# The first batch's row scatters without their marks: an FFT and mixture-of-experts kernel on one core

## The chip, the core and the metric

The kernel runs on one core of a Trainium2 chip. The metric is the device time of one execution in microseconds (us), the median over the runs shown. The core has a matrix engine (TensorE, PE in the rows; its weight loads are PEld), a vector engine (VectorE, DVE), a scalar engine (ScalarE, ACT), a general engine (GpSimd, POOL) and a queue engine (SyncE, SP). Each engine works through its own list of instructions in order and waits for the others by semaphores. DMA transfers are issued by SP and by POOL in this kernel and run on 16 DMA engines.

## What is computed

```python
# x: 8 batches x 2496 positions x 256 channels
X = np.fft.fft(np.fft.fft(x, axis=1), axis=2).real       # 19968 tokens of 256
logits = X @ w_gate + modality_bias[modality_id]          # 8 experts
e_idx = np.argmax(logits, axis=1)
gate_w = softmax(logits)[e_idx]
for e in range(8):
    mask = e_idx == e
    h = np.maximum(X[mask] @ w1[e], 0.0)                  # 256 -> 1024
    out[mask] = gate_w[mask, None] * (h @ w2[e])          # 1024 -> 256
```

## The kernel before

**Three strands of work share the engines.** (1) The transform, batch by batch (b = 0 to 7): loads `XM`, folds on VectorE (L402, L499 to L511), small matrix products into PSUM tiles `psf` (`stage1` L556 and L558, `stage23` L582 to L604), copies out of them (`T`, L524, L532, L533, L594), rows `rp` of a pair of frequencies and their mirrored rows `rm` (`Group.data`, L222 and L223), each 3 x 516 values of 16 bits for 117 partitions. (2) The weights: 16 loads of 1 MB (`wa`, L977), squares for a bound (`wj`, `wst`, L988), a scale (`web`, `wsc`), a split into a high and a low half-precision part (`w`, L1020 on ScalarE and L1021 on VectorE), and a store back to memory (L972). (3) The experts' blocks: 128 or 256 tokens of one expert, `psm` <- `xT`, `w` (L1236, four PSUM tiles of twelve products for 256 tokens), their two halves `H` (ScalarE L1241, then VectorE L1242), `pso` <- `w`, `H` (L1259; the pool has one buffer), the scaled result `ob` (L1266) and a scatter of it to `out` by POOL (L1267).

**Routing.** `route` takes the logits of a batch and gives each row its place `dsti` among its expert's rows (L745). A row then gets its token number and gate value as a `tail` of four 16-bit values (`Group.rows`, two copies at L235 for a group of up to three rows). `scatter` (L817) writes one column of a group, 117 rows, to its places in the table `xd` in memory, by an indirect DMA on POOL. A batch has 22 scatters. Batch 0 is routed in two parts, after 6 and after all 11 of its row columns, which gives 12 and 10 scatters. A block reads its tokens from `xd` by a DMA transpose on SP (`xT`, L1220) and a small load (`ig`, L1223), which wait until all scatters of the batches in question have landed (`drain`). The first three blocks of 128 tokens, named here by their experts 0 to 2, take their rows from SBUF by a one-hot product instead (`onchip`, L798) and don't read `xd`; the fourth is the first that does.

**Who sends the scatters.** In the first stretch (up to the end of the list `SEQ` in `fft_moe`) a scatter goes out through `paced`: one call after each step of the transform and after each half block, and behind a half block that `SEQ` names up to three more as long as the next scatter is of batch 0. `paced` takes the next scatter and adds a dependency on `self.mark`, the latest VectorE instruction of the kind "low half of a product read from PSUM" that the program had written by then (`evac` L533 or `H` L1242). It then calls `rows()` of the group that comes next, so that its tail copies stand in VectorE's list. Later batches use `trickle`, or `paced` with the same marks.

**What sets the order.** The order in which instructions stand on each engine is not written by hand. The program is recorded, and a scheduler with its own model of times lays the instructions out by their dependencies, so a dependency more or less also moves instructions on engines that it doesn't name. POOL's DMAs use eight completion counters in turn: each DMA waits until the one eight before it has landed.

The construction that the diff touches is printed here with its callers.

Of the kernel before, what the change touches and what calls it, by code (L numbers as in the profile page):

```python
# [239 lines left out]
class Pads:  # L240

    b, list = B - 1, None
# [8 lines left out]
class Kernel:  # L251
# [590 lines left out]
    def paced(self):  # L842

        if not self.pend:
            return
        mark = self.mark
        self.next_scatter()
        self.tc.add_manual_dep(self.scattered, mark.name, mybir.DependencyInfo(
            mybir.DependencyClass.Sync, mybir.DependencyReason.DATA), reason="spreads the scatters in time")
        for group, _ in self.pend[:1]:  # L850
            group.rows()

# [589 lines left out]
```

## Time and profile before

| what | before |
|---|---|
| median of 3 runs | 1032.28 us (1031.05 to 1039.42) |
| the profiled execution | 1028.82 us |
| its span, first to last instruction | 1026.8 us |
| TensorE matmul busy, share of the span | 994.3 us, 97% |
| VectorE busy | 560.1 us, 55% |
| ScalarE busy | 446.3 us, 43% |
| POOL busy | 375.9 us, 37% |

The profiled execution is one run; its span leaves 2.0 us outside (start and end). A busy time is the union of an engine's instructions. Matrix products overlap their neighbours in the records, so a busy PE may still be a waiting one, and its waits are read from the rows that give idle time. In a row of the timeline the bracket says how long the engine stood idle before the instruction and which instruction's signal ended that by the trace's inference; where an instruction had other waits too, the name is that of the last to come.

### The profile page before, as it was taken

The page shows a single profiled execution, that of the slowest core. Times are in us where ns is not written, and L with a number is a line of the kernel's source. Part 1 is how long each engine was busy: PE and PEld are TensorE (multiplying, and loading weights), DVE is VectorE, ACT ScalarE, POOL GpSimd, SP SyncE. Part 2 cuts the span into 40 slices and gives each one's busy share as a digit, 9 for nine tenths or more (in the row PEclk, how much of TensorE's full clock was granted, in tenths as well). Part 3 has the DMA queues.
Part 4 walks back from the last instruction along what each step waited for, and adds up shares of the span by engine and source line. Part 5 has one row for each costly group of instructions (what it writes and reads, how often), then busy time and mean ns, then how long its engine had stood idle before and what let it go on. Part 6 is the DMA issues. An engine that isn't in the chain of part 4 may idle for free.

```text
span 1026.8 us, 26338 instructions
## 1 busy us (share of the span) xinstructions
PE 994.3 (97%) x10033; PEld 896.7 (87%) x10033; DVE 560.1 (55%) x1670; ACT 446.3 (43%) x890; POOL 375.9 (37%) x353
## 2 busy tenths in 40 slices
PE   8688999999999999999999999999999999999996
PEld 5587988899999999998999899988888888899995
DVE  4996989675878744955375634553232222222221
ACT  6776788444445333533353333333232323223331
POOL 0245384355245343443344243334444212121111
PEclk9989999999999999999999999999999999999999
DMA  9777997699599798549764954879797986597870
GB/s 333 286 276 261 240 389 255 189 335 308 198 323 265 230 290 208 146 130 308 223 160 132 288 151 111 238 220 255 207 269 220 349 238 160 167 320 137 209 210 22
DMA packets 152018, 237.66 MB, mean 231 GB/s; under 512 B 115820, under 2 KB 118901, under 8 KB 133709
## 3 DMA queue, kind: packets, MB, share of 16 engines
q1 hardware_dynamic: 132509, 193.75, 64.6%
q0 software_dynamic: 19376, 42.16, 13.0%
q8 instruction: 81, 1.33, 0.5%
q14 instruction: 52, 0.43, 0.1%
HBM read 206.37 MB, written 60.48 MB: 260 GB/s over the span
## 4 chain that ended last, share of the span: by engine, by line
PE 80%; issue 6%; DMA 5%; DVE 4%; ACT 2%; POOL 2%; SPq 0%; POOLq 0%; DVEq 0%; ACTq 0%
PE pso L1259 37%; PE psm L1236 36%; PE psf L582 2%; DMA xd<-rm,dsti 2%; PE psf L602 2%; PE psf L556 2%; DMA wa<-w 1%; POOL out L1267 1%; POOL xd L817 1%; DMA XM<-x 1%; ACT wj L988 1%; DVE w L1021 1%; ACT w L1020 1%; DMA ig<-xd 1%; PE psf L587 0%
## 5 line engine op out<-in xcount | busy, mean ns | idle before, releaser
L1236 PE MATMUL psm<-xT,w 128*128 128x256 f16 (+1 forms) x4512 | 457.7, 258 | 5.1 <-ACT xT L801 1.5
L1259 PE MATMUL pso<-w,H 128*128 128x256 f16 x3864 | 451.4, 273 | 0.6 <-ACT ob L1266 0.6
L1236 PEld LDWEIGHTS <-w 128*128 128x128 f16 x4512 | 386.8, 98 | 43.9 <-issue 4.6
L1259 PEld LDWEIGHTS <-H 128*128 128x128 f16 x3864 | 374.0, 98 | 43.6 <-issue 0.7
L1242 DVE SCALAR_TENSOR_TENSOR H<-psm,H 128x512 f16<-128x512 f32 x322 | 219.9, 688 | 322.8 <-ACT H L1241 322.6
L1267 POOL DMA_INDIRECT out<-ob,ig x161 | 165.4, 1028 | 432.8 <-ACT ob L1266 372.2
L1241 ACT ACTIVATE H<-psm 128x512 f16<-128x512 f32 x322 | 190.8, 598 | 237.1 <-PE psm L1236 235.7
L1266 ACT ACTIVATE ob<-pso,gs 128x256 f32<-128x256 f32 x161 | 69.2, 471 | 259.1 <-PE pso L1259 241.4
L817 POOL DMA_INDIRECT xd<-rp,dsti x88 | 99.1, 1126 | 127.3 <-issue 29.8
L817 POOL DMA_INDIRECT xd<-rm,dsti x88 | 99.8, 1134 | 56.1 <-issue 18.9
L533 DVE SCALAR_TENSOR_TENSOR T<-psf,T 120x280 f16<-120x280 f32 (+2 forms) x95 | 43.2, 464 | 70.2 <-ACT T L532 70.1
L532 ACT ACTIVATE T<-psf 120x280 f16<-120x280 f32 (+2 forms) x95 | 38.6, 424 | 8.5 <-PE psf L582 5.1
L988 ACT ACTIVATE wj<-wa 128x1024 uint8<-128x1024 f32 x32 | 34.1, 1065 | 8.1 <-DMA wa<-w 8.0
L602 PE MATMUL psf<-T,pack 120*117 120x145 f16 x330 | 33.5, 224 | 0.0
L582 PE MATMUL psf<-pack,T 128*120 128x144 f16 (+1 forms) x330 | 32.2, 230 | 0.0
L1021 DVE SCALAR_TENSOR_TENSOR w<-wa,wsc,w 128x1024 f16<-128x1024 f32 (+1 forms) x16 | 28.9, 1807 | 2.4 <-ACT w L1020 2.4
L602 PEld LDWEIGHTS <-pack 120*117 120x117 f16 x330 | 27.9, 133 | 0.6
L587 PE MATMUL psf<-m2u,T 128*120 128x280 f32 x88 | 25.5, 418 | 1.9 <-DVE web L411 1.1
L582 PEld LDWEIGHTS <-T 128*120 128x120 f16 x330 | 26.9, 133 | 0.5
L402 DVE TENSOR_TENSOR XM<-XM 128x1280 f32<-128x1280 f32 (+2 forms) x18 | 23.7, 1337 | 6.4 <-DMA XM<-x 6.4
L604 PEld LDWEIGHTS psf<-T,pack 120*117 120x117 f32 x132 | 19.5, 188 | 8.1 <-ACT T L524 4.3
L604 PE MATMUL psf<-T,pack 120*117 120x145 f32 (+1 forms) x132 | 22.8, 296 | 2.9 <-ACT T L524 1.4
(216 smaller groups left out, 664.2 us busy)
## 6 DMA issues: line engine op xcount, KB each, us to landing
w<-w SPq DMA_DIRECT2D x87, 1028.0 KB
w<-w SPq DMA_DIRECT2D x87, 1024.0 KB
XM<-x SPq DMA_DIRECT2D x14, 1280.0 KB
wa<-w SPq DMA_DIRECT2D x16, 1024.0 KB
out<-ob,ig POOLq DMA_INDIRECT x161
XM<-x SPq DMA_DIRECT2D x2, 768.0 KB
xT<-xd SPq DMA_TRANSPOSE x91
xd<-rp,dsti POOLq DMA_INDIRECT x88
```

Source lines behind the costliest of these rows:

```text
L533: self.mark = self.nc.vector.scalar_tensor_tensor(dst[:, 1], ps, scale, dst[:, 0], ALU.mult, ALU.subtract).ins
L582: nc.tensor.matmul(oh, T1[h][:, a, g, :], self.m2h[h][:, w], start=h + k == 0, stop=h * k == 2, skip_group_check=True)
L602: nc.tensor.matmul(ps3[0:M3, cols], self.e3h[:, a, j, :], T2[:, w, cols], start=k == 0, stop=k == 2)
L604: nc.tensor.matmul(ps3[0:M3, cols], self.e3[:, j, :], T2[:, cols], start=True, stop=True)
L817: i = self.nc.gpsimd.indirect_dma_start(out=self.t["xd"], out_offset=bass.IndirectOffsetOnAxis(ap=at, axis=0), in_=row, in_offset=None, bo ...
L988: nc.scalar.activation(jk, x, AF.Square, accum_out=st[:, i:i + 1])
L1236: l1 = nc.tensor.matmul(ps[:, q, :], w1v[:, h, kt, ft], xT[:, xs, :], start=k == 0, stop=k == 5).ins
L1241: nc.scalar.activation(H[:, 0, f0:f0 + NF, :], ps, AF.Relu)
L1242: self.mark = V.scalar_tensor_tensor(H[:, 1, f0:f0 + NF, :], ps, 0.0, H[:, 0, f0:f0 + NF, :], ALU.max, ALU.subtract).ins
L1259: nc.tensor.matmul(po[:, tg, :], H[:, hh, ft, tg * P:(tg + 1) * P], w2v[:, wh, ft, :], start=k == 0, stop=k == 23)
L1266: self.ob = nc.scalar.activation(ob, po[:, tg, :], AF.Identity, scale=gs[:, tg:tg + 1]).ins
L1267: ins = nc.gpsimd.indirect_dma_start(out=t["out"], out_offset=bass.IndirectOffsetOnAxis(ap=ig.bitcast(I32)[:, tg, 0:1], axis=0), in_=ob, i ...
```

## The change

`paced` still takes one scatter per call, at the same calls, and still lets `rows()` of the next group follow. Only where the scatter is of batch 0 it no longer adds the dependency on the mark.

```diff
-        mark = self.mark
+        mark, b = self.mark, self.pend[0][0].b
         self.next_scatter()
-        self.tc.add_manual_dep(self.scattered, mark.name, mybir.DependencyInfo(
-            mybir.DependencyClass.Sync, mybir.DependencyReason.DATA), reason="spreads the scatters in time")
+        if b:
+            self.tc.add_manual_dep(self.scattered, mark.name, mybir.DependencyInfo(
+                mybir.DependencyClass.Sync, mybir.DependencyReason.DATA), reason="spreads the scatters in time")
```

From L848 on the changed kernel's lines are one higher (L1242 before is L1243 in it). The lists of the five engines are the same, but for that shift, up to the first block that reads `xd` on TensorE (about 100 us into the run) and from about 200 us on; POOL's differ from its first scatter on.

POOL's list from its first scatter, before (names: `xd<-rp,dsti` and `xd<-rm,dsti` are scatters, `out<-ob` the results of a block; the number after `ig` tells the blocks apart):

```order
L817 DMA xd<-rp,dsti 162048x516 x3
L817 DMA xd<-rm,dsti 162048x516 x3
L817 DMA xd<-rp,dsti 162048x516 x3
L817 DMA xd<-rm,dsti 162048x516 x4
L817 DMA xd<-rp,dsti 162048x516 x2
L817 DMA xd<-rm,dsti 162048x516 x2
L1267 DMA out<-ob,ig_575 19968x256
L1267 DMA out<-ob,ig_762 19968x256
L817 DMA xd<-rp,dsti 162048x516 x2
L817 DMA xd<-rm,dsti 162048x516 x2
L817 DMA xd<-rp,dsti 162048x516
```

and in the changed kernel:

```order
L817 DMA xd<-rp,dsti 162048x516 x3
L817 DMA xd<-rm,dsti 162048x516 x3
L817 DMA xd<-rp,dsti 162048x516 x3
L817 DMA xd<-rm,dsti 162048x516 x3
L1268 DMA out<-ob,ig_575 19968x256
L817 DMA xd<-rp,dsti 162048x516 x2
L817 DMA xd<-rm,dsti 162048x516 x3
L817 DMA xd<-rp,dsti 162048x516 x2
L817 DMA xd<-rm,dsti 162048x516 x2
L1268 DMA out<-ob,ig_762 19968x256
L817 DMA xd<-rp,dsti 162048x516
```

Both lists hold the 22 scatters of batch 0. The first block's result (`ig_575`) moved from behind seventeen of them to behind twelve, and the second block's (`ig_762`) from behind seventeen to behind twenty-one.

TensorE's list at the end of the block `H_1540` (the third that reads `xd`), before. `pso<-w_2_125,H_1540` is that block's second product, `psf<-m2q,T_1716` a step of the transform, `psm<-xT_2169` the first product of the block after next:

```order
L1259 LDWEIGHTS H_1540
L1259 MATMUL pso<-w_2_125,H_1540 128x256
L593 MATMUL psf<-m2q,T_1716 120x2x80 x2
L1259 LDWEIGHTS H_1540
L1259 MATMUL pso<-w_2_125,H_1540 128x256
L1259 LDWEIGHTS H_1540
L1259 MATMUL pso<-w_2_125,H_1540 128x256
L1259 LDWEIGHTS H_1540
L1259 MATMUL pso<-w_2_125,H_1540 128x256
L1236 LDWEIGHTS w_1_121
L1236 MATMUL psm<-xT_2169,w_1_121 128x256
```

and in the changed kernel:

```order
L1260 LDWEIGHTS H_1540
L1260 MATMUL pso<-w_2_125,H_1540 128x256
L592 MATMUL psf<-m2p,T_1715 120x2x72
L593 MATMUL psf<-m2q,T_1716 120x2x80 x2
L1260 LDWEIGHTS H_1975
L1260 MATMUL pso<-w_0_123,H_1975 128x256
```

Eight products of the next block (`H_1975`) into the one `pso` buffer now stand ahead of the first product of `xT_2169`; before, 24 of those came first.

ScalarE's list from the first `H` of the block `H_1975`, before (`w<-wa` and `w<-wf` are weight splits, `wj` squares, `T` copies of the transform):

```order
L1241 ACTIVATE H_1975<-psm 128x512
L1020 ACTIVATE w_0_123<-wa,wsc 128x2048
L1241 ACTIVATE H_1975<-psm 128x512
L524 COPY T_1715<-psf 128x11x36
L1020 ACTIVATE w_1_121<-wf,wsc 128x1024
L1020 ACTIVATE w_1_121<-wa,wsc 128x1024
L524 COPY T_1715<-psf 128x11x24
L524 COPY T_1716<-psf 128x11x36
L1241 ACTIVATE H_1975<-psm 128x512
```

and in the changed kernel:

```order
L1242 ACTIVATE H_1975<-psm 128x512
L1021 ACTIVATE w_0_123<-wa,wsc 128x2048
L1021 ACTIVATE w_1_121<-wf,wsc 128x1024
L1021 ACTIVATE w_1_121<-wa,wsc 128x1024
L524 COPY T_1715<-psf 128x11x36
L524 COPY T_1715<-psf 128x11x24
L1021 ACTIVATE w_1_124<-wa,wsc 128x2048
L989 ACTIVATE wj,wst<-wa 128x1024
L524 COPY T_1716<-psf 128x11x36
L1242 ACTIVATE H_1975<-psm 128x512
```

The second `H` of that block moved from behind one weight split to behind four and a square. The result `ob` of the block `H_1540` comes, in both lists, after the four `H_1975`, four weight splits, four copies `T` and two squares; before, two more copies (`L594`) stood ahead of it.

## Rows read from the trace of the kernel before

**Rows 1.** The page: engines' busy time, and the granted clock in 40 slices.
```profile
PE 994.3 (97%) x10033; PEld 896.7 (87%) x10033; DVE 560.1 (55%) x1670; ACT 446.3 (43%) x890; POOL 375.9 (37%) x353
PEclk9989999999999999999999999999999999999999
```
**Rows 2.** Stretches: busy time (instructions) of PE, PEld, DVE, ACT, POOL; clock, DMA.
```profile
40.00:60.00 20.00, 15.07 (x230) 14.51 (x231) 19.60 (x60) 14.22 (x24) 7.68 (x6) 0.91 0.52 189
60.00:80.00 20.00, 17.21 (x200) 15.78 (x198) 18.76 (x72) 14.08 (x23) 11.57 (x8) 0.91 0.90 321
...
121.20:132.90 11.70, 11.70 (x111) 10.75 (x110) 11.70 (x41) 11.70 (x18) 8.65 (x6) 1.00 1.04 318
...
400.00:500.00 100.00, 100.00 (x989) 90.54 (x987) 59.62 (x177) 40.46 (x83) 38.89 (x37) 1.00 0.69 204
```
**Rows 3.** POOL's timeline: start, us, what, [idle before <- what ended it].
```profile
45.48 2.30 POOL L817 DMA_INDIRECT xd<-rp,dsti  x1 [18.06 <-DVE rm L235]
...
54.06 0.99 POOL L817 DMA_INDIRECT xd<-rm,dsti  x1 [0.30 <-issue]
66.30 0.99 POOL L817 DMA_INDIRECT xd<-rp,dsti  x1 [11.25 <-DVE pcv L812]
...
72.29 3.01 POOL L817 DMA_INDIRECT xd<-rm,dsti  x1 [0.30 <-issue]
...
78.08 1.11 POOL L817 DMA_INDIRECT xd<-rm,dsti  x1 [0.30 <-issue]
...
94.84 1.25 POOL L817 DMA_INDIRECT xd<-rp,dsti  x1 [0.82 <-DMA out<-ob,ig]
```
**Rows 4.** VectorE's timeline: tail copies, the second part's places, two weight splits.
```profile
40.19 0.15 DVE L235 COPY rm<-tail 117x6 int32<-117x6 int32 x1
...
45.22 0.15 DVE L235 COPY rm<-tail 117x6 int32<-117x6 int32 x1
...
57.83 2.34 DVE L1021 SCALAR_TENSOR_TENSOR w<-wa,wsc,w 128x2048 f16<-128x2048 f32 x1
...
74.04 0.15 DVE L745 CAST dsti<-dst 117x10 int32<-117x10 f32 x1
...
74.58 2.33 DVE L1021 SCALAR_TENSOR_TENSOR w<-wa,wsc,w 128x2048 f16<-128x2048 f32 x1
```
**Rows 5.** SP's timeline of DMA issues: two weight loads, the first transpose.
```profile
43.07 2.06 SPq L977 DMA_DIRECT2D wa<-w  x1
...
99.35 1.32 SPq L1220 DMA_TRANSPOSE xT<-xd  x1
...
135.59 0.45 SPq L977 DMA_DIRECT2D wa<-w  x1
```
**Rows 6.** TensorE's timeline: the waits behind which the argument stands, and one place between.
```profile
102.19 2.84 PE L1236 MATMUL psm<-xT,w 128*128 128x128 f16 x48 [0.61 <-DMA xT<-xd]
...
131.00 2.78 PE L1236 MATMUL psm<-xT,w 128*128 128x256 f16 x24
...
147.57 0.16 PE L422 MATMUL psf<-wst,ones 128*128 128x1 bf16 x1 [1.13 <-ACT wj L988]
...
162.33 0.51 PE L592 MATMUL psf<-m2p,T 128*120 128x144 f32 x2 [0.94 <-DVE xeb L411]
...
164.47 0.83 PE L1236 MATMUL psm<-xT,w 128*128 128x256 f16 x6 [0.92 <-DVE xsc L413]
```
**Rows 7.** ScalarE's timeline.
```profile
50.62 1.06 ACT L988 ACTIVATE wj<-wa 128x1024 uint8<-128x1024 f32 x1 [2.08 <-DMA wa<-w]
...
131.31 0.73 ACT L594 COPY T<-psf 120x280 f32<-120x280 f32 x2
...
132.92 0.54 ACT L1266 ACTIVATE ob<-pso,gs 128x256 f32<-128x256 f32 x1
...
146.37 1.06 ACT L988 ACTIVATE wj<-wa 128x1024 uint8<-128x1024 f32 x1 [2.15 <-DMA wa<-w]
```
**Rows 8.** DMA from 40 to 100 us: POOL's queue, packets, MB, share of 16 engines.
```profile
q0 software_dynamic: 1504, 2.84, 14.0%
```

## The prediction

> **What bounds the kernel now.** I read the page first, then the stretches, then the waits of TensorE one by one, and last what POOL does.
>
> TensorE is busy 994.3 of 1026.8 us [rows 1]. Busy is not yet working at its pace, but in the stretch from 400 to 500 us it is busy throughout at the full clock while VectorE has 59.6 and ScalarE 40.5 us of work in 100 [rows 2], and its timeline shows no wait there. So whatever happens early, from about 200 us on the rest is a fixed amount of matrix work. The change can move the end only by what it does to TensorE's waits before that. They lie early: in 40 to 60 us TensorE is busy 15.1 of 20 us, in 60 to 80 us 17.2, at a mean clock of 0.91 [rows 2]. Behind 100 us four waits are worth naming: 0.61 us for the first transposed tokens at 102.19, 1.13 us for a product over weight squares at 147.57, 0.94 us at 162.33 and 0.92 us at 164.47 [rows 6]. Together 3.6 us. That is the first thing to see: a gain beyond about 10 us has nowhere to come from in the stretch that the change can reach.
>
> Now POOL. The first scatter of batch 0 starts at 45.48, the sixth at 54.06, the seventh at 66.30 after 11.25 us of idle time, the thirteenth at 78.08, the last at 94.84 [rows 3]. Two of these waits are marks: the first scatter's group had its tail copies at 40.19 and the second group's at 45.22 [rows 4], 5 and 21 us before its first scatter went out. SP issues the first transpose at 99.35 [rows 5], 3.3 us behind the end of the last scatter's instruction (94.84 + 1.25 = 96.09), and TensorE takes it up at 102.19, 2.8 us later [rows 6].
>
> **What the change does, step by step.**
>
> *The scatters go out sooner.* The first six can start behind the copy at 40.19 + 0.15, five us sooner, the second six behind the first instead of at 66.30, so twelve are out near 60 us instead of 78. The second part's ten can't start before their places, cast at 74.04 + 0.15 [rows 4]; before, their first went at 78.08 because POOL was still busy with the first part. From 74.2, with the first held up to about 77 as the one at 72.29 was, then nine scatters and one block result at 1.3 us (the pitch of a 0.99 us scatter with the 0.30 us between two, [rows 3]), the last ends at 77 + 10 x 1.3 = 90 us, and 91 with one more held up. That is 5 us sooner than 96.1.
>
> *What the 5 us are worth.* The transpose follows the last landing, so TensorE could have its tokens at about 102.2 - 5 = 97. It arrives for them at 101.58 (102.19 less 0.61) and its list before that place is unchanged, so it can gain 0.61 us and no more. **Term 1: -0.6** (bounds -0.6 and 0). The other 4.4 us are slack. If the scatters came out no sooner than before, that term would be 0.
>
> *The scatters' packets.* POOL's 24 DMAs from 40 to 100 us (22 scatters, 2 results) took 14.0% of 16 DMA engines [rows 8], 0.14 x 60 / 24 = 0.35 us of all engines each. The load of weights at 43.07 [rows 5] is late already: ScalarE stood 2.08 us for it until 50.62 [rows 7]. About three scatters more fall in front of its landing, so it can come 0 to 3 x 0.35 = 1.0 us later, and ScalarE has little slack there. The DMA engines are busy only 0.52 of the stretch, so I take less than half. **Term 2: +0.4** (0 to +1.0). The other end gains nothing: from 60 to 80 us the engines are 0.90 busy [rows 2] and six scatters leave that stretch, but none of TensorE's waits there is for a load.
>
> *VectorE beside POOL.* More scatters now lie beside VectorE's long instructions. In the trace the scatter is the one that pays: 3.01 us at 72.29 instead of 0.99 [rows 3], while the weight split at 74.58, with a scatter across its start and another one inside, took 2.33 us, and the same one at 57.83 with no scatter near it 2.34 [rows 4]. **Term 3: 0.** The Trainium skill, SBUF — State Buffer, section "Who interferes with whom", says that the two engines lock a shared port pair for a whole instruction and that whichever issues first blocks the other; by that rule scatters could also hold VectorE up. The rows agree for one direction only. Its further inference, that an operation with two SBUF inputs doesn't hold up descriptor writing, is not what the 3.01 us suggest.
>
> *The lists that the scheduler moved.* The dependency that is gone moved work between 100 and 200 us on TensorE, VectorE and ScalarE; each list keeps the same work. Two places matter. At the first, TensorE now has eight products of `H_1975` ahead of the products of `xT_2169`. They need the one `pso` buffer, so they wait for `ob` of the block before, on ScalarE. Before, ScalarE needed from the first `H_1975` (just before 121.20) to that `ob` at 132.92 [rows 7] 11.7 us without a gap (busy 11.70 of 11.70 us, [rows 2]). In the new list the same instructions stand ahead of it, less the two copies of 0.73 us, so 11.0 us, and its own half us makes 11.5: with the 0.6 us of term 1 it is done at 121.2 - 0.6 + 11.5 = 132.1. TensorE came to this place at 131.00 [rows 6], so now at 130.4, and stands 1.7 us. Before, the 24 products covered this. If ScalarE loses as much again to VectorE's small steps the wait is 3.4, if the copies in front also shorten it is 0. **Term 4: +1.7** (0 to +3.4).
>
> At the second, the two products over weight squares at 147.57, one behind the other's 18 block products, now stand together, and their two squares stand closer on ScalarE too. The squares wait for the load issued at 135.59 [rows 5, 7]. With the transpose that stood in front of that load issued up to 2 us sooner, the wait can vanish (-1.1); with the load landing at the same time, TensorE waits for the second square, about 1.8 us instead of 1.13 (+0.7). Between them: **term 5: -0.2** (-1.1 to +0.7).
>
> The two waits at 162.33 and 164.47 are for VectorE's chain over the next batch's input, which doesn't start on TensorE, so a TensorE that comes later waits less: half of the 1.9 us is taken off. **Term 6: -0.9** (-1.9 to 0).
>
> *Sum*: -0.6 + 0.4 + 0 + 1.7 - 0.2 - 0.9 = +0.4 us, from -3.6 to +5.1 by the bounds. On the profiled execution's own time that is 1028.8 + 0.4 = 1029.2 (its span and the 2.0 us around it). The median of the runs shown is 1032.28, 3.5 above the profiled one, and the runs themselves lie from 1031.05 to 1039.42; so the time to expect of a median is 1032.28 + 0.4 = **1032.7**.
>
> **The rivals.** *(a) The early scatters pay off as hoped.* If all four waits behind 100 us go, because the transposes, and behind them the loads on SP's queue, come 5 us sooner, the gain is 3.6 us: 1028.7. For it: SP stands for those landings with loads queued behind. Against it: the next weight load on SP's list waits for a weight split on VectorE, not for the transposes. *(b) The load at 43.07 becomes the limit and the new order makes it worse*: all upper bounds, +1.0 + 3.4 + 0.7 = +5.1 us: 1037.4. *(c) VectorE is held up by the scatters, and the kernel is slower.* In 40 to 60 us VectorE is busy 19.6 of 20 us [rows 2], and twelve scatters now go out there instead of six. Each that starts ahead of a VectorE instruction and blocks it for its 0.99 us would cost that much, twelve of them 12 us, all of it on the chain to TensorE: 1044. It decides as soon as more than ten of twelve do so. This is what the skill's rule on the shared port pair gives if POOL issues first; against it stand the 2.33 and 2.34 us. *(d) The change does nothing*: the scatters are held by their landings (each waits for the one eight before) instead of the marks. Then only the moved lists count, +0.6 us: 1032.9. The seventh scatter's 11 idle us, which no landing of an earlier scatter can explain, speak against it.
>
> **How the numbers follow.** My forecast (moved waits that cancel within 2 us) gets 0.52, (d) 0.08, (a) 0.18, (b) 0.15, (c) 0.04, and 0.03 is left for a gain above 1% by a way that I don't see, such as the low clock of the first 80 us going away with its waits. The range from 1027 to 1039 takes in all but (c), the unseen gain and the outer ends of (a) and (b), about 0.88 by my chances; it is as wide as (a), (b) and the runs' own spread make it. About 1% (10.3 us) is what a measurement of this kernel can tell from no change: below 1022.0 is faster, 0.03; above 1042.6 slower, 0.05; the rest the same, 0.92.
>
> **What would show it.** Right: scatters of batch 0 from about 40 us on, twelve out by 60 us, the last ended near 90; the first transpose near 94 and no wait of TensorE for it; a new wait of 1 to 3 us in front of the first `pso` of `H_1975` near 131; TensorE as full as before from 200 us on. Wrong: the last scatter still at 95 (terms 1 and 2 fall); VectorE's weight splits longer than 2.34 us beside scatters (then (c)); ScalarE standing past 52 us for the load of 43.07 (then (b)); waits of TensorE that sum before 200 us to over 5 us more or less than now.

## The result: 0.57% slower, just outside the predicted range

| what | before | changed |
|---|---|---|
| median of the runs | 1033.15 us (1029.25 to 1039.42) | 1039.05 us (1036.90 to 1046.45) |
| ratio | 1 | 1.0057, 95% interval 1.0043 to 1.0072 |
| the profiled execution | 1028.82 us | 1040.54 us |
| its span | 1026.8 us | 1038.6 us |

The forecast was 1032.7 us in a range up to 1039.0. It called the change the same within 1%, and that it is; but it saw +0.4 us where +5.9 came, and the time lies 0.05 us above the range. The base of the forecast, a median of three runs, lay 0.87 us below that of all 21, so those 0.05 us decide little; but +5.9 also lies above +5.1, the upper bound of the prediction's sum. The two profiled executions are 11.7 us apart, twice the distance of the medians, because the one of before (1028.82) is faster than any of the runs listed and the one of the changed kernel is 1.5 us above its median. So a microsecond in one of the two traces is not yet a microsecond of the change.

The page of the changed kernel (busy us, share of the span, instructions; below it the clock in 40 slices) answers to [rows 1]. TensorE's work is the same, and it is spread over a longer span:

```profile
PE 999.8 (96%) x10033; PEld 901.2 (87%) x10033; DVE 561.7 (54%) x1670; ACT 445.8 (43%) x890; POOL 382.9 (37%) x353
PEclk9989999999999999999999999999999999999998
```

The stretches of the changed kernel (busy time and instructions of PE, PEld, DVE, ACT, POOL, then TensorE's granted clock, DMA share, GB/s), to be read beside [rows 2]:

```profile
40.00:60.00 20.00, 14.00 (x208) 13.44 (x209) 18.75 (x60) 13.96 (x25) 16.02 (x11) 0.91 0.53 184
60.00:80.00 20.00, 16.99 (x206) 16.16 (x204) 17.04 (x64) 12.87 (x20) 9.96 (x4) 0.83 0.88 315
80.00:100.00 20.00, 17.57 (x97) 14.03 (x95) 12.50 (x43) 10.97 (x26) 9.86 (x10) 0.93 0.86 298
100.00:120.00 20.00, 18.07 (x182) 16.33 (x181) 16.12 (x45) 13.17 (x25) 3.06 (x2) 0.90 0.48 132
120.00:140.00 20.00, 18.32 (x197) 16.72 (x195) 19.43 (x72) 14.88 (x26) 12.15 (x7) 1.00 1.03 297
```

and the same view of before, for the stretches that were not shown:

```profile
80.00:100.00 20.00, 17.84 (x98) 13.85 (x96) 12.40 (x39) 11.14 (x27) 12.53 (x11) 1.00 0.82 293
100.00:120.00 20.00, 19.31 (x252) 18.25 (x251) 18.82 (x60) 13.97 (x27) 4.15 (x3) 1.00 0.77 221
120.00:140.00 20.00, 20.00 (x186) 18.37 (x185) 18.53 (x67) 16.97 (x31) 14.54 (x11) 1.00 1.05 319
```

TensorE is less busy in each stretch from 40 to 140 us, and from 60 to 120 us its clock is lower as well: 0.83, 0.93 and 0.90 against 0.91, 1.00 and 1.00. A share below 1.00 is time at the lower level, 1.2 instead of 2.4 GHz, and in 20 us these three differences are worth at most (0.08 + 0.07 + 0.10) x 20 = 5.0 us of work at the full clock. The prediction had priced waits and no clock. Most of these 5.0 us belong to the two executions and not to the change, as far as the mean clocks of whole runs tell. Where the changed kernel ran beside the one before on another chip (f_after below), its 12 runs had a granted clock of 0.9826 in the mean and the 35 of before 0.9828; on a further chip it was 0.9824 (a_nopause) against 0.9850. Over such a run that is 0.2 and 2.7 us. (The two profiled executions had 0.993 and 0.987.)

The rest of the distance between the two traces is standing of TensorE: from 40 to 100 us it is busy 48.56 us against 50.13 in before, from 100 to 300 us 191.45 against 196.31. In this pair more of it lies behind 100 us, in the stretch of the moved lists, than before it.

What POOL did (timeline: start, us, what, idle before and what ended it), beside [rows 3]:

```profile
40.93 4.20 POOL L817 DMA_INDIRECT xd<-rp,dsti  x1 [13.18 <-DVE rm L235]
...
62.53 4.12 POOL L817 DMA_INDIRECT xd<-rm,dsti  x1 [0.31 <-issue]
...
77.39 3.30 POOL L817 DMA_INDIRECT xd<-rp,dsti  x1 [5.56 <-DVE xeb L412]
...
91.61 0.99 POOL L1268 DMA_INDIRECT out<-ob,ig  x1 [0.30 <-issue]
101.07 2.07 POOL L817 DMA_INDIRECT xd<-rp,dsti  x1 [8.47 <-DMA out<-ob,ig]
```

The first part went as forecast: scatters from 40.9 us, the twelfth at 62.53 instead of at 75.60 and earlier than the thirteenth's 78.08 of before. The second part did not: it starts at 77.39, because its places come at 76.93 and not at 74.04 [rows 4] (VectorE had stood until 71.33 for a wait that ended at 68.40 in before), and its last scatter stands 8.47 us for the landing of the block result right ahead of it. So the last scatter goes out 6.2 us later than before (94.84), not 5 us sooner.

ScalarE, VectorE and SP of the changed kernel, one row each for the load of 43 us, for the first wait on a store, for the places and for the first transpose [rows 4, 5, 7]:

```profile
51.82 1.06 ACT L989 ACTIVATE wj<-wa 128x1024 uint8<-128x1024 f32 x1 [2.94 <-DMA wa<-w]
```
```profile
71.33 0.15 DVE L411 TENSOR_SCALAR web<-psf 128x1 f32<-128x1 f32 x1 [2.96 <-issue]
...
76.93 0.15 DVE L745 CAST dsti<-dst 117x10 int32<-117x10 f32 x1
77.47 2.33 DVE L1022 SCALAR_TENSOR_TENSOR w<-wa,wsc,w 128x2048 f16<-128x2048 f32 x1
```
```profile
105.06 1.32 SPq L1221 DMA_TRANSPOSE xT<-xd  x1
```

And TensorE's waits (timeline; beside [rows 6]):

```profile
71.53 0.19 PE L422 MATMUL psf<-nst,ones 128*128 128x1 bf16 x2 [2.90 <-DVE web L411]
...
107.74 4.37 PE L1237 MATMUL psm<-xT,w 128*128 128x128 f16 x48 [1.29 <-DMA xT<-xd]
...
139.47 1.03 PE L1260 MATMUL pso<-w,H 128*128 128x256 f16 x8 [1.58 <-ACT ob L1267]
...
147.06 0.71 PE L1237 MATMUL psm<-xT,w 128*128 128x256 f16 x5 [0.66 <-DVE H L1243]
...
155.90 0.18 PE L422 MATMUL psf<-wst,ones 128*128 128x1 bf16 x1 [0.15 <-DVE wsc L413]
156.92 0.16 PE L422 MATMUL psf<-wst,ones 128*128 128x1 bf16 x1 [0.84 <-ACT wj L989]
...
191.98 1.25 PE L1260 MATMUL pso<-w,H 128*128 128x256 f16 x10 [1.49 <-DVE w L1022]
...
261.57 0.22 PE L602 MATMUL psf<-T,pack 120*117 120x145 f16 x1 [1.28 <-ACT T L532]
```

The 48 products at 107.74 took 4.37 us where before they took 2.84: TensorE had stood 1.29 us, and from 107.60 to 111.00 us its granted clock was 0.50.

### The profile page after: what moved, and what is told of

The parts are those of the page before. It is cut to its first block, busy times and chain, and to the rows that moved or that the text cites. A ratio compares the mean times of both kernels' runs of the same rounds, so it can differ in the third digit from the quotient of the medians.

```text
span 1038.6 us, 26336 instructions
## 1 busy us (share of the span) xinstructions
PE 999.8 (96%) x10033; PEld 901.2 (87%) x10033; DVE 561.7 (54%) x1670; ACT 445.8 (43%) x890; POOL 382.9 (37%) x353
## 4 chain that ended last, share of the span: by engine, by line
PE 65%; issue 5%; DMA 3%; POOL 2%; DVE 1%; SPq 1%; ACT 0%; POOLq 0%; DVEq 0%; ACTq 0%
PE pso L1260 31%; PE psm L1237 30%; PE psf L582 2%; PE psf L602 2%; PE psf L556 1%; POOL out L1268 1%; DMA xd<-rp,dsti 1%; DMA xd<-rm,dsti 1%; DMA out<-ob,ig 1%; POOL xd L817 1%; DMA ig<-xd 0%; SPq L1221 0%; DVE H L1243 0%; ACT T L532 0%; DVE tb_cum L1126 0%
## 5 line engine op out<-in xcount | busy, mean ns | idle before, releaser
L1243 DVE SCALAR_TENSOR_TENSOR H<-psm,H 128x512 f16<-128x512 f32 x322 | 219.8, 688 | 326.2 <-ACT H L1242 325.5
L1268 POOL DMA_INDIRECT out<-ob,ig x161 | 162.5, 1009 | 436.2 <-ACT ob L1267 367.3
L1242 ACT ACTIVATE H<-psm 128x512 f16<-128x512 f32 x322 | 190.4, 598 | 235.1 <-PE psm L1237 232.3
L817 POOL DMA_INDIRECT xd<-rm,dsti x88 | 108.9, 1237 | 57.8 <-DVE H L1243 18.4
L989 ACT ACTIVATE wj<-wa 128x1024 uint8<-128x1024 f32 x32 | 33.9, 1059 | 10.6 <-DMA wa<-w 10.4
```

The source lines that it names most:

```text
L817: i = self.nc.gpsimd.indirect_dma_start(out=self.t["xd"], out_offset=bass.IndirectOffsetOnAxis(ap=at, axis=0), in_=row, in_offset=None, bo ...
L1242: nc.scalar.activation(H[:, 0, f0:f0 + NF, :], ps, AF.Relu)
L1243: self.mark = V.scalar_tensor_tensor(H[:, 1, f0:f0 + NF, :], ps, 0.0, H[:, 0, f0:f0 + NF, :], ALU.max, ALU.subtract).ins
L1268: ins = nc.gpsimd.indirect_dma_start(out=t["out"], out_offset=bass.IndirectOffsetOnAxis(ap=ig.bitcast(I32)[:, tg, 0:1], axis=0), in_=ob, i ...
```

## The experiments

**How they are built.** The change has two halves: POOL no longer waits for the marks, and the scheduler then lays the five lists out differently. To part them, some kernels hold each engine's list in the order of the other kernel by edges of order only, which make no engine wait. `PIN` holds the instructions' names engine by engine, to a little past the last place where the two kernels' lists differ:

```diff
+def pin(nc, tc):
+    at = {i.name: i for i in nc.all_instructions()}
+    for names in PIN.values():
+        names = [f"I-{n}" for n in names.split() if f"I-{n}" in at]
+        for a, b in zip(names, names[1:]):
+            tc.add_manual_dep(at[b], a, mybir.DependencyInfo(
+                mybir.DependencyClass.NoSync, mybir.DependencyReason.DATA), reason="order")
```

Kernels that stand together below ran together on one chip with the kernel before, and each ratio is to that. The chips differ (before took 1033.6 us on one, near the 1033.15 of the first comparison, and 1051.6 to 1059.5 us on four slower ones), so only ratios are compared between them. Three theories were on trial: **P**, the wait in front of the last scatter costs; **L**, the packets of the early scatters hold up a weight load and a weight store; **O**, the moved lists cost.

### The wait in front of the last scatter

`pause` makes a DMA of POOL wait for the one two before it in the program's order, after four in a row. Between two scatters the program drops that edge, as it drops every order among writes to the table `xd`; between a block result and a scatter it stays. The first attempt took it from the wrong scatters (those of the first part):

```diff
-            self.tc.add_manual_dep(ins, self.sent[-3].name, mybir.DependencyInfo(
-                mybir.DependencyClass.Sync, mybir.DependencyReason.DATA), reason="a pause in the queue")
+            kind = mybir.DependencyClass.Sync if b else mybir.DependencyClass.NoSync
+            self.tc.add_manual_dep(ins, self.sent[-3].name, mybir.DependencyInfo(
+                kind, mybir.DependencyReason.DATA), reason="a pause in the queue")
```

> The changed kernel with the same five lists; only the pause of a batch 0 scatter (a wait for the landing of the DMA two before it in the program's order, here the block result that POOL issues right ahead of the last scatter) is no longer waited for. Theory P (that pause is what costs): in the changed kernel the last scatter stood 8.47 us for it (92.6 to 101.07); without it the last scatter starts near 93, the first transpose near 97, and TensorE finds its tokens there. It saves the 1.29 us of waiting at 107.74 and the 1.5 us that the low clock behind it cost, so 2.8 us of the 5.9 between the medians: near 1036.2, and more if the later waits go too. Theory L (the early scatters' packets hold up a weight load and a weight store before 72 us): no more than the 1.29 us of that one wait goes, 1038. Theory O (the moved lists behind 110 us): the waits behind 110 us stay, 1037 to 1038.

It left the last scatter's wait in place (7.92 us, to 101.59) and the lists as they were, so it says nothing about P and serves as another measurement of the changed kernel: 1.0056 (1.0029 to 1.0083).

The second attempt frees the last scatter; the changed kernel itself ran beside its repetition:

```diff
-        self.pause(i.ins)
+        self.pause(i.ins, b)
...
-        if self.inrow > ROW_MAX:
+        if self.inrow > ROW_MAX and b < 2:
+            self.inrow = 1
+        elif self.inrow > ROW_MAX:
```

> The changed kernel with its five lists, and the last scatter of batch 0 really freed of the wait for the landing of the block result ahead of it (all pauses of batch 0's scatters are left out). Theory P (the pause costs): last scatter near 93, first transpose near 97, tokens before TensorE comes for them; 3 us faster than the changed kernel, about 1.0025 times the time of before. Theory L (early packets hold up loads and stores): the early loss stays and only the short wait of 1.3 us goes; 1.004 to 1.005. Theory O (moved lists): waits behind 110 us stay, 1.003 or more.

> The changed kernel itself, beside the next three on the same chip. Both halves of the change are in it: scatters out early and lists moved. 1.005 to 1.006 times the time of before, as measured elsewhere (1.0057).

> The changed kernel with the last scatter of batch 0 freed of its wait for a block result's landing (a second measurement of a_free). Theory P: 2 to 3 us faster than f_after. If the wait is slack, because TensorE comes late to the transposed tokens in any case, the same as f_after within 1.5 us.

a_free 1.0087 (1.0053 to 1.0122); f_after 1.0044 (1.0014 to 1.0074) and f_free 1.0055 (1.0030 to 1.0081) on one chip. POOL's last scatter in f_after, then in f_free:

```profile
103.61 1.00 POOL L817 DMA_INDIRECT xd<-rp,dsti  x1 [7.69 <-DMA out<-ob,ig]
```
```profile
97.08 1.00 POOL L817 DMA_INDIRECT xd<-rp,dsti  x1 [0.30 <-issue]
```

It comes 6.5 us sooner, and the kernel is no faster: the medians are 1065.73 and 1066.19 us. But the first transpose, which waits for landings, comes only 1 us sooner. SP in f_after, then in f_free:

```profile
106.38 1.32 SPq L1221 DMA_TRANSPOSE xT<-xd  x1
```
```profile
105.33 1.33 SPq L1223 DMA_TRANSPOSE xT<-xd  x1
```

So this edit moved the scatter and hardly the tokens. What speaks against P here is TensorE: it takes up the tokens without a wait in both, at 109.47 us in f_after and at 112.01 in f_free, and f_after's ratio is 1.0044 all the same. a_free, on another chip, is no faster either. Intervals of 0.3% don't exclude P's 2 to 3 us by themselves; P finds no support. From the other side comes l_pool, the kernel before with its marks, where only POOL's list is the changed kernel's.

```diff
-PIN = {"POOL": before, "SP": before, "ACT": before, "PE": before, "DVE": before}
+PIN = {"POOL": changed, "SP": before, "ACT": before, "PE": before, "DVE": before}
```

> The kernel before with marks; only POOL's list is the changed kernel's (first block result earlier, second one right ahead of the last scatter, which then waits for its landing near 101 us); the four other lists are before's. Theory P: 1.002 to 1.003. Theory O with the place on TensorE, ScalarE and VectorE: 1.000 to 1.001.

1.0007 (0.9980 to 1.0033, so at most 3.4 us), although TensorE stood for its tokens in that execution:

```profile
103.09 5.20 PE L1237 MATMUL psm<-xT,w 128*128 128x128 f16 x48 [4.59 <-DMA xT<-xd]
```

Its last scatter (97.39) waited 1.73 us only, and TensorE had come to this place at 98.5 instead of 101.6 us, so this run bounds the cost of POOL's order, not that of a late last scatter by itself. (Some twenty of TensorE's rows late in the run also stand differently in it.)

### Each half by itself

The early scatters alone (the changed source with the five lists of before) and the moved lists alone (the source of before with the five lists of the changed kernel), each on three chips:

```diff
     with tile.TileContext(nc, schedule_with_timeline_sim=True) as tc:
         fn(tc, t)
+        pin(nc, tc)
```

> The five lists of the kernel before, with the marks of batch 0 not waited for: the scatters go out early and nothing else moves. Theory P: the block result stands five places ahead of the last scatter, not right ahead of it, so the pause costs about nothing and the time is that of before, 1033. Theory L: the load that ScalarE waits for until 50.62 comes 0.9 us later, and the store that VectorE waits for until 68.40 comes 1.7 us later, as in the changed kernel; 1.5 to 2.6 us slower, 1034.7 to 1035.8. Theory O: nothing moved, so 1033.

> The five lists of the changed kernel, with the marks of batch 0 waited for as before: only the lists moved. Theory L: the early scatters are gone, so 1033 to 1034 if nothing else costs. Theory O: the wait of 1.7 us for ob near 138 and the others behind 110 us stay, +2.7 to +4.7 us: 1036 to 1038. Theory P: the last scatter still stands for the landing of the block result right ahead of it, first transpose near 103 or later, so the tokens come 3 us or more late: 1036 to 1038 too, but with the wait at the first transposed tokens in the trace.

> The lists of before, batch 0's marks not waited for (a second measurement of b_lists): the early scatters alone. Theory L (packets of the early scatters hold up a load and a store that ScalarE and VectorE wait for): +2 to +5 us, 1.002 to 1.005. Theory O (the moved lists are the whole loss): 1.000 to 1.001.

> The lists of the changed kernel, batch 0's marks waited for (a second measurement of a_marks): the moved lists alone. Theory O: +3 to +4 us by the waits between 100 and 200 us, 1.003 to 1.004. Theory L: 1.000 to 1.001. If both halves cost and add, f_after is the sum of the two; if one covers the other, f_after is near the larger.

> The early scatters alone once more (lists of before, marks of batch 0 not waited for), for a third interval beside the one with the scatters behind the load. Theory L with the load issued at 43 us as the place: ScalarE gets that load 0.8 to 0.9 us later (its wait 2.9 instead of 2.1 us) and the time is 1.002 to 1.004. If the loss is only in further stalls of TensorE behind late signals near 50 us, seen in some traces, and none is there: 1.000 to 1.001.

> The moved lists alone once more (lists of the changed kernel, marks of batch 0 waited for). Theory O: TensorE's lost time from 100 to 200 us 6 to 10 us against 4.4 in before, a wait for ob of 1.5 to 3 us near 138, 1.003 to 1.005. If POOL's order and the pause were the place, l_pool would have shown it: 1.000 to 1.001.

The moved lists also ran without the pause:

> The lists of the changed kernel, marks of batch 0 waited for, no pause for batch 0's scatters: the moved lists alone. Theory O: the loss of the run with marks stays, 1.0035. Theory P: the first transpose comes near 97 instead of 103.7 and the loss goes, 1.000 to 1.001. Theory L: with the marks there is no early loss in either, so whatever is left is the lists' or the pause's.

| | chip 1 | chip 2 | chip 3 | chip 4 |
|---|---|---|---|---|
| both halves (the changed kernel) | 1.0056 (a_nopause) | 1.0044 (f_after) | | 1.0087 (a_free, no pause) |
| early scatters alone | 1.0049 (b_lists) | 1.0038 (f_early) | 1.0041 (e_early) | |
| moved lists alone | 1.0035 (a_marks) | 1.0048 (f_lists) | 1.0045 (e_lists) | 1.0064 (am_free, no pause) |

Each ratio in the first three columns is uncertain by 0.2 to 0.4%, and every interval lies above 1. Their means are 1.0043 for either half (4.5 us of the 1052 to 1059 us there) and 1.0050 for both, well below the sum of the halves. So each half costs on these chips, and together they cost hardly more than one: part of what one loses, the other loses anyway. Chip 4 alone (1.0064 and 1.0087, intervals that overlap) would not tell that from a sum. That both halves cost had no theory of mine by itself. O is right for the moved lists; L is right that the early scatters cost, though not on how, as shown below. On a chip of the faster kind, to which the first comparison's belongs by its time, neither half ran alone.

The runs' clocks part the two halves further. With the early scatters alone the mean granted clock is 0.0016 to 0.0020 below that of before in each of the three measurements, 1.7 to 2.1 us of a run and so about two fifths of what they cost. With the moved lists alone it is 0.0008 below, 0.0004 above and 0.0008 above: their cost is not in the clock.

### Where the early scatters cost

Marks dropped for the first six scatters only, and for the second six only (lists of before):

```diff
-        if b:
+        n = self.nsent = getattr(self, "nsent", 0) + 1
+        if b or n > 6:
```
```diff
-        if b:
+        n = self.nsent = getattr(self, "nsent", 0) + 1
+        if b or n <= 6 or n > 12:
```

> The lists of before, and only the first six scatters of batch 0 freed of their marks (they start near 41 instead of 45.5 us; the next six still wait for theirs near 66). Theory L: the load that ScalarE waits for until 50.6 comes up to 0.9 us later, the store that VectorE waits for until 68.4 comes at its time; 1.001. If the loss of the run with all marks dropped (1.0049) comes from the start of scatters beside the load, it is here in full: 1.004 or more.

> The lists of before, and only the second six scatters freed of their marks (they go out right behind the first six, from 55 instead of 66 us). Theory L: the load at 50.6 comes at its time, the store that VectorE waits for comes 1.7 to 3 us later (near 70 to 72) and TensorE stands as much longer before the second part of the transform; 1.002 to 1.004. If the load is what counts: 1.000.

1.0032 (1.0007 to 1.0056) and 1.0009 (0.9979 to 1.0040). The first six, which start at 40.3 instead of 45.8 us, do cost; for the second six the interval holds nothing as well as 0.4%. L had expected the larger cost from the second six. Then the first scatter was put behind the weight load issued at 43 us, once with the marks (late6) and once without (late12; the lists of before in both, but for some twenty of TensorE's rows far behind 200 us in late12):

```diff
 def pin(nc, tc):
     at = {i.name: i for i in nc.all_instructions()}
+    tc.add_manual_dep(at["I-469"], "I-912", mybir.DependencyInfo(
+        mybir.DependencyClass.Sync, mybir.DependencyReason.DATA), reason="behind a weight load")
```

> The kernel before with its lists and marks, and one more wait: the first scatter of batch 0 also waits for ScalarE's first square of the weights loaded at 43.07 us (50.6 us), so that the first six go out from about 51.8 instead of 45.5 us, behind that load. Theory L (scatters' packets beside a load delay it): the load comes 0 to 1 us sooner, ScalarE's wait of 2.08 us shrinks by that, and the time is 0 to 1.5 us below before: 0.9985 to 1.000. Rival (late scatters cost, as the marks do): the second six still start at 66, so nothing gets later than in before, and the time is the same; slower by over 0.1% only if the store that VectorE waits for near 68 is held up, 1.001 to 1.002.

> The lists of before without batch 0's marks, but the first scatter waits for the same square of weights (50.6 us): the first twelve go out in one row from 51.8 to about 68 us. Theory L, the load at 43.07 as the place: near before, 1.000 to 1.001, against 1.0042 for the scatters that start at 41. Theory L, the store at 60 us as the place: twelve scatters lie beside it, so as bad as all early, 1.003 to 1.005.

late6 1.0004 (0.9977 to 1.0031), late12 1.0000 (0.9973 to 1.0026). In late12 twelve scatters go out in a row from 51.66 us, and the time is that of before, within 0.27%. Its rows for the load on ScalarE and for the wait on the store on TensorE, and the latter in before:

```profile
50.19 1.06 ACT L989 ACTIVATE wj<-wa 128x1024 uint8<-128x1024 f32 x1 [2.01 <-DMA wa<-w]
```
```profile
69.49 0.19 PE L422 MATMUL psf<-nst,ones 128*128 128x1 bf16 x2 [2.50 <-DVE web L411]
```
```profile
68.60 0.19 PE L422 MATMUL psf<-nst,ones 128*128 128x1 bf16 x2 [1.17 <-DVE web L411]
```

The second row is the other place that L named. TensorE stood 2.5 us there, more than the 1.2 us of before, and the time shows no cost of it. a_memset points the same way: the changed kernel with the instruction that waits for the store moved in VectorE's list behind a weight split, which takes this wait away.

```diff
-L1029 MEMSET w_1_124 128x7
 L411 TENSOR_SCALAR web<-psf 128x1
...
 L1022 SCALAR_TENSOR_TENSOR w_2_122<-wa,wsc,w_2_122 128x1024
+L1029 MEMSET w_1_124 128x7
```

> The changed kernel with one instruction moved in VectorE's list: the clearing of the seven pad words of a weight buffer (L1029), which waits until the store of the old weights has landed (71.3 us), stands 27 instructions later, behind the next weight split. Theory L: the 2.90 us that TensorE stood before 71.53 shrink by 1.7 or more, the second part of the scatters starts up to 2 us sooner, and the low clock from 70.0 us goes: 1.7 to 2.6 us faster than the changed kernel, 1036.4 to 1037.3. Theories P and O: the waits behind 100 us take that up again, 1039.

1.0048 (1.0018 to 1.0078), no different from the changed kernel's 1.0056 on that chip, though L's 1.7 to 2.6 us would be hard to see in such intervals; in its trace neither `web` nor the product behind it waits any more. All this points to the time of the load at 43 us as the place, and not to the store; it does not show it. A caution: the early scatters alone did not run on the chip of late12, which is of the faster kind; that they cost there too is inferred from three slower ones.

What happens beside the load is seen where TensorE's first waits lie. ScalarE of e_lists (scatters from 45.4 us), then of e_early (from 40.4 us), each with the second half of the first block and the first square of the load:

```profile
47.88 0.60 ACT L1242 ACTIVATE H<-psm 128x512 f16<-128x512 f32 x1 [0.74 <-PE psm L1237]
50.71 1.06 ACT L989 ACTIVATE wj<-wa 128x1024 uint8<-128x1024 f32 x1 [2.24 <-DMA wa<-w]
```
```profile
51.52 0.60 ACT L1242 ACTIVATE H<-psm 128x512 f16<-128x512 f32 x1 [3.91 <-remote]
52.01 1.05 ACT L989 ACTIVATE wj<-wa 128x1024 uint8<-128x1024 f32 x1
```

TensorE in e_lists and in e_early, at the products that both wait for and at its next work:

```profile
45.00 2.84 PE L1237 MATMUL psm<-xT,w 128*128 128x128 f16 x48 [1.47 <-ACT xT L801]
...
51.95 0.50 PE L798 MATMUL psf<-Pt,rp 117*128 117x128 f16 x6 [2.30 <-DVE Pt L782]
```
```profile
44.90 2.84 PE L1237 MATMUL psm<-xT,w 128*128 128x128 f16 x48 [1.58 <-ACT xT L801]
...
58.48 0.80 PE L798 MATMUL psf<-Pt,rp 117*128 117x128 f16 x6 [8.89 <-issue]
```

In e_early the 48 products are recorded up to 47.74, but ScalarE, which waits for nothing else, starts on them at 51.52. VectorE then stands for a product recorded up to 49.5, and TensorE, which waits for VectorE, stands 8.89 us:

```profile
56.59 0.17 DVE L807 COPY pcv<-psf 128x6 f32<-128x6 f32 x1 [3.36 <-remote]
```

It is the signal that is late: the trace has the updates of TensorE's semaphore for the two halves at 46.99 and 51.49 us in e_early, at 46.51 and 47.85 in e_lists. The load is not: the square at 52.01 starts right behind the late `H` without a wait, and by the semaphore of its queue the load lands 6.9 to 7.9 us behind its issue in the nine traces with scatters from about 40 us on these four chips, 6.9 to 7.6 in the five others. So L's mechanism, a load that ScalarE stands longer for, is not what costs there. Two other causes fall by the trace: the granted clock is 1.00 from 44 to 50 us in both, and no fetch of instructions is under way, since the queues that carry them move no packet between 44.1 and 64.1 us in e_early. All those nine traces have the late `H` (50.15 to 55.17 us, 2.2 to 6.3 behind the recorded end of its products), and none of the ten with scatters from 44.95 us or later (47.42 to 48.58; five of these ran on the same four chips). TensorE is then busy 8.2 to 12.4 of the 20 us from 40 to 60, against 13.5 to 15.5. b_first6 has it and costs, b_second6 has not and shows no cost. The one trace of the changed kernel on the chip of the first comparison doesn't have it: `H` at 48.28, only the load 0.86 us later.

### Where the moved lists cost

TensorE's list of the changed kernel in the kernel before, all other lists as they were:

```diff
-PIN = {"POOL": before, "SP": before, "ACT": before, "PE": before, "DVE": before}
+PIN = {"POOL": before, "SP": before, "ACT": before, "PE": changed, "DVE": before}
```

> The kernel before with marks; only TensorE's list is the changed kernel's (eight products of H_1975 into the one pso buffer ahead of the products of xT_2169, and the other moves between 100 and 200 us); ScalarE, VectorE, POOL and SP keep before's lists. Theory O with the place on TensorE: a wait for ob of 1.7 us or more near 132 to 138, and +2 to +4 us, 1.002 to 1.004 (ScalarE has two more copies ahead of that ob than in the changed kernel, so perhaps more). If the loss is in the fit of all lists to the marks' times: 1.000 to 1.001.

1.0130 (1.0100 to 1.0160), more than all of the change. Its waits of TensorE:

```profile
136.13 1.03 PE L1260 MATMUL pso<-w,H 128*128 128x256 f16 x8 [3.21 <-ACT ob L1267]
155.08 0.16 PE L422 MATMUL psf<-wst,ones 128*128 128x1 bf16 x1 [2.07 <-ACT wj L989]
163.29 1.48 PE L1237 MATMUL psm<-xT,w 128*128 128x256 f16 x12 [1.68 <-DVE H L1243]
173.18 0.39 PE L1237 MATMUL psm<-xT,w 128*128 128x256 f16 x2 [2.93 <-ACT w L1021]
```

Here ScalarE still has its old order, so the `ob` comes later than in the changed kernel: 3.21 us, near the 3.4 of term 4's upper end. With ScalarE's new list it is 1.58 us, and it is 1.58 us in each of the nine traces that have the changed kernel's lists and were read there, on the four slower chips and in the first comparison. From 100 to 200 us TensorE is busy 93.2 us in the mean of these nine (91.4 to 95.6) and 95.6 in that of the nine with the lists of before (93.9 to 96.9). These 2.4 us, of which the wait for `ob` is 1.58, are about half of what the moved lists cost. POOL's list alone showed no cost (l_pool), so the place is in the other engines' lists. (Of the second nine, l_pool has before's lists but for POOL's.)

## Why the prediction was wrong, step by step

Two steps failed, one for each half. Term 2 priced the early scatters as the delay of one load, so that terms 1 to 3 came to -0.2 us; by themselves they cost 0.43% on the slower chips, where the load is not late and TensorE's signals are. And "Two places matter" priced the moved lists at +0.6 us (terms 4 to 6); by themselves they cost 0.43% there too.

- **"The last ends at ... 90 us."** Wrong, by 13 us (101.07 + 2.07 = 103.1), and the sign named for that, "the last scatter still at 95", came. Two things were missed. The second part was to start from 74.2, but its places come at 76.93, since VectorE is itself late. And "nine scatters and one block result at 1.3 us" overlooked that the last scatter waits for a landing. The sign stood in a row that I used, [rows 3]: 0.82 us at 94.84, ended by `out<-ob`. In before that result stood five places ahead, in the new list it stands right ahead, and the order in front shows this. **Term 1** so had the wrong sign: the wait at the tokens grew from 0.61 to 1.29 us. Nor does the transpose follow the last scatter as closely as the 3.3 us of before: in f_free it comes 7 us behind its end (97.08 + 1.00, 105.33). But by f_after, which has the cost without that wait, and by l_pool it decides little.
- **Term 2, the load at 43.07.** +0.4 within 0 to 1.0; the trace has 0.86. As a delay of the load the bounds hold. What they left out is what the runs on the four slower chips found: signals of TensorE that come 2 to 6 us late beside it. The early half costs about 4.5 us there instead of the -0.2 of terms 1 to 3. I also had no term for the weight store that VectorE waits for near 68 us, because the row put that wait down to a product of TensorE that had long been done; it grew from 1.12 to 2.96 us, and late12 and a_memset show no cost of it.
- **Term 3, VectorE beside POOL.** Right: the weight split with scatters beside it takes 2.33 us as before, and the scatter pays, 4.20 us for the first one that starts in VectorE's busy stretch. The Trainium skill, SBUF — State Buffer, section "Who interferes with whom", has the lock hold whichever engine comes second, where VectorE is in a two-port mode; here too only POOL is seen to wait. The prediction's doubt about that section's inference on two SBUF inputs is not settled by its 3.01 us: a scatter also reads its places `dsti` from SBUF. Rival (c) falls.
- **Term 4, the wait for `ob`.** Right: +1.7 forecast, 1.58 measured, at the place named.
- **Term 5, the two products over weight squares.** Right in size: -0.2 forecast; 0.15 + 0.84 = 0.99 instead of 1.13. The forecast was the middle of two opposite cases, so this is in part luck.
- **Term 6.** The two waits at 162 and 164 went altogether (-1.9, the far bound), but others of the same size came at 147.06, 191.98 and 261.57 us (0.66, 1.49, 1.28), for VectorE and ScalarE. So "from about 200 us on the rest is a fixed amount of matrix work" did not hold at 261.57 either. The step that failed is "Two places matter": I priced the waits that I could name and took the rest of the moved rows as even. The moved lists alone cost about 4.5 us on the slower chips, not +0.6.
- **The clock** had no term, and from 60 to 120 us the trace has up to 5.0 us of it. By the means of whole runs the change itself lost 0.2 us of clock on one chip and 2.7 on another.
- **The rivals.** (b), all upper bounds, 1037.4 us, was nearest to what came, for reasons that hold in part: the stretch beside the load and the new order cost, but the load was 0.86 us later in the first comparison's trace and not late on the four slower chips. It had 0.15. (d) falls, the marks did hold the scatters. The range ended at 1039.0 because (b) was the far end that I took in; the rows of the moved lists that I had not priced had no share in it, and a chain of small terms of both signs hid that only the losses among them could grow.

Open remains why TensorE's signals come late beside the load, why the trace of the first comparison shows no such delay while its ratio is the same, and which rows of the moved lists besides the one at `ob` carry their cost. For the first comparison's own chip the split into two halves is not shown.

## What to carry to other kernels

A wait that spaces transfers may protect what runs beside a large load: before it is dropped, look for a load that an engine stands for at that time, and try the transfers behind it (late12 dropped the marks and showed no loss, on the faster kind of chip). A dependency removed in a program that a scheduler lays out is two changes; pin the old lists to learn what each is worth, since here each alone cost nearly what both did. And a wait seen in one trace, even of 4.6 us, is worth what it costs when taken away, not its length.

## What had not been expected

- **Landing of a small result.** The block result issued at 91.61 us had landed only when the last scatter could start, at 101.07: 9.5 us for 128 rows of 1 KB. Before, it was 85.97 to 94.84, 8.9 us. The Trainium skill, DMA: Bandwidth & Descriptors, section "Anatomy of one DMA — SWDGE (gpsimd) path", gives 2.0 us plus the bytes divided by 436,000 per us, an estimate of 2.3 us for this size; the trace differs, in a stretch where the DMA engines are 0.86 busy.
- **Late signals of TensorE**, 2.2 to 6.3 us behind the recorded end of the first block's products, in nine of nine traces with scatters from about 40 us on four chips. The profile calls what ended such a wait "remote", "issue", or another product that had ended.
- **A cost that is less than the sum of its parts**: 0.43% for either half, 0.50% for both on the slower chips.
